# Storing attention rows one round later, interleaving the load halves, and starting the weight loads at round 18

## The chip, the cores and the metric

The kernel runs on one core of one Trainium2 chip. Its five engines work side by side and meet through semaphores: TensorE (PE, matrix products; its weight loads are listed apart as PEld), VectorE (DVE), ScalarE (ACT), GpSimd (POOL) and SyncE (SP), which here only issues DMAs. The metric is the device time of one execution in microseconds (us). The kernel before has a median of 1035.58 us over three runs (1028.32, 1035.58 and 1047.32).

## The reference

The program is a chunked attention followed by two mixture-of-experts layers.

1. Attention: 4 batches, 8 heads, 768 tokens, head size 64, in float32. Each chunk of 32 queries sees 8 memory keys, 16 keys to the left of the chunk, its own 32, and 8 to the right; softmax with scale 1/8; then the weighted sum of the values.
2. The result, as 3072 tokens of 512 numbers, goes through a noisy top-2 router (8 experts, `x @ w1[e]`, relu, `@ w2[e]`, inner size 1024) and the two experts' outputs are added with their weights.
3. That goes through a second layer of 8 experts, with one expert for each token.

## The kernel before, in words

**Tiles and rounds.** The 3072 tokens are cut into 24 tiles of 128. The attention is a software pipeline of 26 rounds, the loop over `t` in `build` (a "round" below is one pass of this loop). Round t does, in this order: `scores(t)` on PE with the maximum and the subtraction on DVE (lines 316 to 325), `flip(t-1)` (PE transposes, copied out by ACT), `exp(t)` on ACT, a piece of `route` (the first router, mostly DVE) in some rounds, `values(t-2)`, `spread(t)` (POOL copies inside the loaded tile), `turn(t-3)` (PE transposes of the finished rows, line 383) and `logits(t-4)`.

**values(t).** PE multiplies the weights with the values (L356). Then SP is given the five loads of tile t+5 (L293), since the tile's buffer is now free: there are five input buffers, `LK = 5`. DVE normalises (L362 to L365) and writes the high half of the row in float16 into a buffer `w`, named x16 (L369, called "the cast" below); POOL writes the low half (L370); SP stores both to `X16` in DRAM (L376, printed as X<-x). There are two x16 buffers, so the cast of tile t writes what tile t-2 used, and it has to wait until the store of tile t-2 has read it.

**Queues.** All these DMAs are issued by SP in program order. An instruction that waits holds back every DMA behind it. The order of the work on every engine is the order in which the Python code emits it. Each SP transfer takes one of eight semaphores in turn (DMAHW0 to DMAHW7 in the order listings) and waits, before it is issued, for the transfer that used that semaphore eight places earlier.

**Weights.** `Weights.fill` loads an expert's weights as eight pieces of 128 x 1024 float32 into four `stage` buffers (L74). From round 24 on, ACT and DVE turn a piece into two float16 halves (L127, L128), which frees its buffer and lets the next load start. The expert products (L543 and L554) follow; their first needs the first pieces of expert 0.

**The first rounds.** Round 2 also makes a table `wide` for the router (DVE), a tile of zeros, and three stores of zeros to `L` and `G` (L1280, L1281).

**The last two tiles** (22 and 23) are not transposed by PE: SP issues a DMA transpose of the row (L373), which needs POOL's half, and then the store.

Of the kernel before, what the change touches and what calls it, by code (L numbers as in the profile page):

```python
# [23 lines left out]
QN, KN, VN = 512, 736, 1040  # L24
QK = QN + KN
VC = VN // 4
XK, XQ, XU, XV = VN, VN + KN, VN + QK, VN + QK + QN
# [227 lines left out]
class Attention:  # L255
# [30 lines left out]
    def load(self, t):  # L286

        x = self.X[t % LK]  # L290
        for i, (p, n, o, e) in enumerate(((0, 32, 0, XU), (32, 32, 3 * VC, XU), (64, 64, XK, XQ),
                                          (64, 32, XU, XV + VN), (96, 32, XU, XV + VC))):
            self.nc.sync.dma_start(x[p:p + n, o:e], self.qkv[i][t])  # L293

    def spread(self, t):
# [48 lines left out]
    def values(self, t):  # L344
        nc, wk, g = self.nc, self.wk, self.g
        x = self.X[t % LK]
        y = self.ET.pop(t)
        o = self.ps.tile([128, 2, 512], F32, name="o")
        for a in range(2):
            for u in range(2):  # L350
                for ch in range(4):
                    i = (D + 1) * (4 * ch + 2 * a + u)
                    v = x[:, i:i + D + 1]
                    v = bass.AP(tensor=v.tensor, offset=v.offset, ap=[v.ap[0], [XV + (3 - 2 * ch) * VC, 2], v.ap[1]])
                    j = 64 * (ch % 2) + 32 * u
                    nc.tensor.matmul(o[32 * ch:32 * ch + 32, a, 130 * u:130 * u + 130],  # L356
                                     y[:, 2 * (ch // 2) + a, j:j + 32], v, start=True, stop=True)
        if t + LK < NT:
            self.load(t + LK)
        o = o[:, :, 0:260].rearrange("p a (h d) -> p a h d", h=4)  # L360
        r = wk.tile([128, 2, 4, 1], F32, name="r")
        nc.vector.tensor_scalar(r, o[:, :, :, D:D + 1], 1e-9, 1.0 / SX, op0=OP.add, op1=OP.mult)  # L362
        nc.vector.reciprocal(r, r)
        x = wk.tile([128, 2, 4, D], F32, name="x", bufs=2)
        nc.vector.tensor_tensor(x, o[:, :, :, 0:D], r.to_broadcast([128, 2, 4, D]), op=OP.mult)  # L365
        xp = x.rearrange("p b a d -> p (b a d)")
        w = g.rr.tile([128, 2, 4, 128], F16, name="x16", bufs=2)
        wf = w.rearrange("p a k q -> p (a k q)")
        nc.vector.tensor_copy(wf[:, :DM], xp)  # L369
        nc.gpsimd.tensor_tensor(wf[:, DM:], xp, wf[:, :DM], op=OP.subtract)  # L370
        y = self.XT[t] = g.rr.tile([128, 2, 4, 128], F16, name="xt", bufs=3)
        if t >= NT - 2:
            nc.sync.dma_start_transpose(out=y.rearrange("p a k q -> p (a k) q"), in_=wf)  # L373
        else:
            self.W[t] = w
        self.stores.append(nc.sync.dma_start(rows(g.X16, t), wf))  # L376

    def turn(self, t):
        nc = self.nc
        w = self.W.pop(t).rearrange("p a k q -> p (a k) q")  # L380
        p = self.ps.tile([128, 512], F32, name="xp").bitcast(F16).rearrange("p (i q) -> p i q", i=8)
        for i in range(8):
            nc.tensor.transpose(p[:, i, :], w[:, i, :], self.g.ident16)
        nc.scalar.activation(self.XT[t].rearrange("p a k q -> p (a k) q"), p, AF.Copy)
# [129 lines left out]
def rows(x, t):  # L514

    return x.rearrange("(u p t) d -> u p t d", u=2, t=M)[t // M, :, t % M]
# [712 lines left out]
def build(tc, xa, xb, xc, xd, xe, noise, wr, wg2, w1, w2, v1, v2, out):  # L1229
    nc = tc.nc  # L1230
    with ExitStack() as top:
        top.enter_context(tc.manual_schedule())
        g = G()
# [16 lines left out]
        def src(e):  # L1250
            v = (w1[e].rearrange("(p k) f -> p (k f)", k=4), w2[e].rearrange("(p k) d -> p (k d)", k=8))
            return lambda i, c: v[i][:, c * 1024:c * 1024 + 1024]

        with ExitStack() as ctx:
            wk = ctx.enter_context(tc.tile_pool(name="wk", bufs=2))
            ld = ctx.enter_context(tc.tile_pool(name="ld", bufs=1))
            at = Attention(tc, g, (xa, xb, xc, xd, xe), ld, wk)
            at.ps = ctx.enter_context(tc.tile_pool(name="psa", bufs=1, space=PSUM))
            at.load(0)
            nc.scalar.preload_act_table_set("natural_log_exp_and_others")  # L1260
            gates = at.gates(noise, wr)
            at.clear(0)
            constants(tc, g, ld)
            for t in range(1, LK):
                at.load(t)
            route = None
            for t in range(NT + 2):
                if t + 1 < LK:
                    at.clear(t + 1)
                if t == 0:  # L1270
                    next(gates)
                if t == 3:
                    at.wrh = next(gates)
                if t == 2:
                    g.wide = g.c.tile([128, 128, M], F16, name="wide")
                    nc.vector.tensor_copy(g.wide, g.iota[:, 0:128, None].to_broadcast([128, 128, M]))
                    z = ld.tile([128, NT * E], F32, name="zero")
                    nc.vector.memset(z, 0.0)
                    for u in range(2):
                        nc.sync.dma_start(g.L.rearrange("(u p t) x -> u p (t x)", u=2, p=128)[u], z)  # L1280
                    nc.sync.dma_start(g.G.rearrange("(p t) x -> p (t x)", p=128), z[:, 0:2 * NT])  # L1281
                if t >= 14:
                    W.depth = min(W.depth + 1, 4)
                    if t == 14:
                        for e in range(E):
                            W.add((1, e), src(e))
                    W.fill()
                if t < NT:
                    at.scores(t)
                if 0 < t <= NT:  # L1290
                    at.flip(t - 1)
                if t < NT:
                    at.exp(t)
                if route and t < 25:
                    for _ in range(2 if t in (17,22) else 1):
                        next(route, None)
                if t >= 2:
                    at.values(t - 2)
                if t < NT:
                    at.spread(t)  # L1300
                if 0 <= t - 3 < NT - 2:
                    at.turn(t - 3)
                if t >= 4:
                    at.logits(t - 4)
                if t >= 4 and (t - 4) % TB == TB - 1:
                    route = at.route((t - 4) // TB)
                    next(route)
                if t == 20:
                    m1 = Moe1(tc, g, dr)
                    m1.gather(0)  # L1310
                if t == 22:
                    for b in range(m1.preps(0)):
                        m1.prep(0, b)
                if t >= 24 and W.may():
                    W.high()
                    W.low(nc.vector)
            m1.gates(0)
# [143 lines left out]
def layouts(inp):  # L1461
# [4 lines left out]
    def split(x, y):  # L1466

        return x.reshape(B, 2, 2, 2, *y)

    def pad(a):  # L1470
        p = np.zeros((B, H, S + 40, D), f)
        p[:, :, 16:16 + S] = a
        return p
    q = split(inp["q"], (TB, 4, 32, D)).transpose(0, 4, 2, 7, 6, 1, 3, 5).reshape(NT, 128, QN)
    p = pad(inp["k"])
    k = np.stack([np.concatenate([x for c in range(4) for x in (p[:, :, 128 * j + 32 * c:128 * j + 32 * c + 32],
                                                                 inp["mem_k"])]
                                 + [p[:, :, 128 * j + 128:128 * j + 152]], axis=2) for j in range(TB)], axis=2)
    k = split(k, (TB, KN // 4, D)).transpose(0, 4, 2, 6, 1, 3, 5).reshape(NT, 128, KN)
    p = pad(inp["v"])  # L1480

    def values(w, c):
# [6 lines left out]
    vb = values(np.concatenate([x for j in range(TB) for x in (p[:, :, 128 * j + 128:128 * j + 152], inp["mem_v"])],  # L1489
                               axis=2), 1)  # L1490
    seq = [b * TB + j for b, j in SEQ]
    k, q, va, vb = k[seq], q[seq], va[seq], vb[seq]
    vu = va[:, 32:].reshape(NT, 32, 4, VC)[:, :, ::-1].reshape(NT, 32, VN)
    qkv = [np.concatenate(x, axis=2) for x in ((va[:, 0:32], k[:, 0:32], q[:, 0:32]),
                                               (vb[:, 0:32], k[:, 32:64], q[:, 32:64]), (k[:, 64:],),
                                               (q[:, 64:96], vu), (q[:, 96:], vb[:, 32:]))]

    def rows(w):

        w = w.reshape(E, 4, 128, 128, 8).transpose(0, 2, 1, 4, 3)  # L1500
        return np.ascontiguousarray(w).reshape(E, DM, F)
# [40 lines left out]
```

## Time and profile before

| | us |
|---|---|
| median of three runs | 1035.58 |
| lowest and highest run | 1028.32, 1047.32 |
| profiled execution, its own time | 1033.13 |
| span of its profile | 1031.4 |
| PE busy in that span | 951.9 |
| DVE, ACT, POOL busy | 504.7, 386.3, 479.4 |

The attention takes the first 147 us or so, the first expert layer ends near 670 us, the second takes the rest. The profile's span is 1.7 us shorter than the time of its own execution. A timeline row gives the start (us from the span's start), the duration, the engine, the line, the operation and its operands; "SPq" rows are the issue of a DMA and not its transfer. A bracket at the end gives how long the engine was idle before, and what ended that idle time.

### The profile page before, as it was taken

Reading aid. Unit: us, or ns where it says so; the run is one execution under the profiler, and the core shown is the slowest. Engines: PE = TensorE matmul, PEld = TensorE weight load, DVE = VectorE, ACT = ScalarE, POOL = GpSimd, SP = SyncE. Lnnn points to the kernel's source line nnn. Section 1 sums busy time; section 2 is a strip of 40 time slices with the busy share of each in tenths; the row PEclk is TensorE's granted clock in tenths of the full one; section 3 lists DMA queues with packets and bytes.
Section 4 is the critical chain, followed back from the end, with each engine's and each line's share of the span. In section 5 each row is a group of like instructions: output and inputs, shape, how many; then the busy total and the mean of one; then the engine's idle time right before and its main releaser. Section 6 shows DMA issues by size and latency. Waiting matters only on the chain.

```text
span 1031.4 us, 18755 instructions
## 1 busy us (share of the span) xinstructions
PE 951.9 (92%) x7259; PEld 566.5 (55%) x7259; DVE 504.7 (49%) x1032; ACT 386.3 (37%) x653; POOL 479.4 (46%) x484
## 2 busy tenths in 40 slices
PE   5897868999989999999999999985889999999998
PEld 4786745656545555455554555542457555555665
DVE  7689885642423443244332443473475436565511
ACT  2453444322323343333433343252423345454421
POOL 6755653334545454645546354335522635443421
PEclk9998969999999999999999999988899999999999
DMA  9999959745746686678766676489535879987720
GB/s 214 253 258 256 237 137 273 178 90 121 189 100 172 164 186 158 154 169 190 170 160 162 152 177 143 131 256 194 96 121 147 219 184 263 287 217 211 148 56 19
DMA packets 189218, 180.75 MB, mean 175 GB/s; under 512 B 152148, under 2 KB 153044, under 8 KB 188352
## 3 DMA queue, kind: packets, MB, share of 16 engines
q1 hardware_dynamic: 166736, 131.24, 54.2%
q0 software_dynamic: 21952, 48.07, 15.8%
q8 instruction: 60, 0.98, 0.4%
q14 instruction: 38, 0.31, 0.1%
q10 hardware_dynamic: 432, 0.15, 0.1%
HBM read 118.27 MB, written 39.53 MB: 153 GB/s over the span
## 4 chain that ended last, share of the span: by engine, by line
PE 41%; issue 16%; POOL 8%; DMA 4%; DVE 2%; ACT 0%; POOLq 0%; DVEq 0%; ACTq 0%
PE ph L543 19%; PE py L554 19%; POOL x L1049 2%; POOL xp L1018 2%; POOL out_dram L1068 2%; POOL gs L1018 2%; DMA stage<-in_v_dram 1%; PE py L736 1%; DMA xp<-Y,ter 1%; DMA xp<-Y,tbr 1%; DMA gs<-Pa,ter 1%; DMA out_dram<-y,teo 0%; DVE hT L546 0%; DMA xt<-x 0%; DVE w L128 0%
## 5 line engine op out<-in xcount | busy, mean ns | idle before, releaser
L543 PE MATMUL ph<-xT,w 128*128 128x384 f16 (+3 forms) x2688 | 426.5, 318 | 19.9 <-DVE hT L546 10.4
L554 PE MATMUL py<-w,hT 128*128 128x512 f16 x1800 | 394.2, 379 | 0.0
L543 PEld LDWEIGHTS <-w 128*128 128x128 f16 x2688 | 262.5, 99 | 166.8 <-issue 24.5
L554 PEld LDWEIGHTS <-hT 128*128 128x128 f16 x1800 | 175.7, 98 | 207.0
L546 DVE SCALAR_TENSOR_TENSOR hT<-ph,hT 128x384 f16<-128x384 f32 (+3 forms) x224 | 115.9, 521 | 218.0 <-ACT hT L545 216.9
L128 DVE SCALAR_TENSOR_TENSOR w<-stage,w 128x1024 f16<-128x1024 f32 x128 | 167.2, 1309 | 66.5 <-ACT w L127 66.3
L545 ACT ACTIVATE hT<-ph 128x384 f16<-128x384 f32 (+3 forms) x224 | 103.3, 463 | 212.6 <-PE ph L543 209.0
L127 ACT ACTIVATE w<-stage 128x1024 f16<-128x1024 f32 x128 | 133.6, 1049 | 19.1 <-DMA stage<-in_v_dram 14.3
L654 ACT ACTIVATE y<-py,gs 128x512 f32<-128x512 f32 x48 | 32.9, 686 | 176.4 <-PE py L554 170.3
L657 POOL DMA_INDIRECT L<-l,t3y x43 | 44.5, 1035 | 109.6 <-DVE l L686 106.2
L675 DVE SCALAR_TENSOR_TENSOR x<-y,x 128x512 f16<-128x512 f32 x50 | 34.4, 688 | 123.0 <-ACT x L671 122.9
L657 POOL DMA_INDIRECT Y<-y,t3y x43 | 44.8, 1041 | 91.5 <-ACT y L654 85.7
L1068 POOL DMA_INDIRECT out_dram<-y,tbo x20 | 20.8, 1039 | 110.8 <-ACT y L1067 89.0
L316 PE MATMUL s<-x 128*64 128x64 f32 x768 | 49.6, 287 | 16.3 <-DMA x<-in_xe_dram 11.6
L611 POOL DMA_INDIRECT Y<-ol,late x48 | 56.4, 1175 | 16.4 <-issue 16.4
L316 PEld LDWEIGHTS s<-x 128*64 128x64 f32 x768 | 46.3, 209 | 17.8 <-POOL x L303 8.3
L1067 ACT ACTIVATE y<-py,gs 128x512 f32<-128x512 f32 x27 | 18.6, 687 | 94.8 <-PE py L554 64.1
L370 POOL TENSOR_TENSOR x<-x,x 128x512 f16<-128x512 f32 x24 | 29.4, 1226 | 45.8 <-DVE x L369 25.1
L585 POOL DMA_INDIRECT xg<-X,t3x x43 | 42.0, 976 | 15.1 <-issue 14.6
L585 POOL DMA_INDIRECT gs<-G,t3g x41 | 38.7, 944 | 12.5 <-issue 12.5
L303 POOL COPY x<-x 24x780 f32<-24x780 f32 x48 | 41.0, 855 | 5.2 <-issue 2.5
L1049 POOL TENSOR_TENSOR x<-xp 128x512 f32<-128x512 f32 x27 | 35.9, 1355 | 15.1 <-DVE xg L1052 11.7
(276 smaller groups left out, 708.1 us busy)
## 6 DMA issues: line engine op xcount, KB each, us to landing
stage<-in_w_dram SPq DMA_DIRECT2D x64, 512.0 KB, 4.1
stage<-in_v_dram SPq DMA_DIRECT2D x64, 512.0 KB, 5.1
x<-in_xa_dram SPq DMA_DIRECT2D x24, 286.0 KB, 5.5
X<-x SPq DMA_DIRECT2D x24, 256.0 KB, 4.4
x<-in_xd_dram SPq DMA_DIRECT2D x24, 194.0 KB, 6.7
x<-in_xb_dram SPq DMA_DIRECT2D x24, 188.5 KB, 6.6
x<-in_xc_dram SPq DMA_DIRECT2D x24, 184.0 KB, 6.0
x<-in_xe_dram SPq DMA_DIRECT2D x24, 96.5 KB, 5.6
```

What stands on the lines that cost most here:

```text
L127: nc.scalar.activation(hi, src, AF.Copy, scale=SW)
L128: return lambda v=nc.vector: v.scalar_tensor_tensor(lo, src, SW, hi, op0=OP.mult, op1=OP.subtract)
L316: nc.tensor.matmul(s[o:o + 64, ch // 2, b], q[:, b, ch], k[:, b, 40 * ch:40 * ch + 64], start=True, stop=True)
L543: nc.tensor.matmul(p[:, :n], w1[:, a, k, f, :], xT[:, b, k, :n], start=(i == 0), stop=(i == 11))
L545: nc.scalar.activation(hT[:, 0, f, :n], p[:, :n], AF.Relu)
L546: nc.vector.scalar_tensor_tensor(hT[:, 1, f, :n], p[:, :n], 0.0, hT[:, 0, f, :n], op0=OP.max, op1=OP.subtract)
L554: nc.tensor.matmul(p[:m], hT[:, a, f, o:o + m], w2[:, c, f, :], start=(i == 0), stop=(i == 23))
L585: self.nc.gpsimd.indirect_dma_start(out=out, out_offset=None, in_=src, in_offset=IO(ap=idx, axis=0))
L611: st = nc.gpsimd.indirect_dma_start(out=self.Y, out_offset=IO(ap=idx[:, i:i + 1], axis=0), in_=z, in_offset=None, bounds_check=2 * N - 1, ...
L657: st = nc.gpsimd.indirect_dma_start(out=dst, out_offset=IO(ap=idx, axis=0), in_=src, in_offset=None, bounds_check=2 * N - 1, oob_is_err=False)
L1049: nc.gpsimd.tensor_tensor(s, x[:, :DM], x[:, DM:], op=OP.add)
L1068: st = nc.gpsimd.indirect_dma_start(out=self.out, out_offset=IO(ap=idx, axis=0), in_=y, in_offset=None, bounds_check=N - 1, oob_is_err=False)
```

## The change

1. The store of a tile's rows moves out of `values(t)` into a new method `keep`, which `turn(t)` calls in the next round. For tiles 22 and 23, which have no `turn`, it stays in `values`, behind the DMA transpose.
2. The five loads of a tile are issued in another order, so that they alternate between partitions 0 to 63 and 64 to 127. Their sizes are as before.
3. The table `wide` and the zero stores move from round 2 to round 6.
4. The first weight loads move from round 14 to round 18: one in each of rounds 18 to 21, where it was 14 to 17.

```diff
-        for i, (p, n, o, e) in enumerate(((0, 32, 0, XU), (32, 32, 3 * VC, XU), (64, 64, XK, XQ),
-                                          (64, 32, XU, XV + VN), (96, 32, XU, XV + VC))):
+        for i, (p, n, o, e) in enumerate(((0, 32, 0, XU), (64, 32, XU, XV + VN), (32, 32, 3 * VC, XU),
+                                          (64, 64, XK, XQ), (96, 32, XU, XV + VC))):
             self.nc.sync.dma_start(x[p:p + n, o:e], self.qkv[i][t])
...
         if t >= NT - 2:
             nc.sync.dma_start_transpose(out=y.rearrange("p a k q -> p (a k) q"), in_=wf)
+            self.keep(t, wf)
         else:
             self.W[t] = w
-        self.stores.append(nc.sync.dma_start(rows(g.X16, t), wf))
+
+    def keep(self, t, wf):
+        self.stores.append(self.nc.sync.dma_start(rows(self.g.X16, t), wf))
 
     def turn(self, t):
         nc = self.nc
         w = self.W.pop(t).rearrange("p a k q -> p (a k) q")
+        self.keep(t, w.rearrange("p i q -> p (i q)"))
...
-                if t == 2:
+                if t == 6:
                     g.wide = g.c.tile([128, 128, M], F16, name="wide")
...
-                if t >= 14:
+                if t >= 18:
                     W.depth = min(W.depth + 1, 4)
-                    if t == 14:
+                    if t == 18:
                         for e in range(E):
                             W.add((1, e), src(e))
```

On SP, in the first rounds: the loads of tile 7 (buffer x_90) and the store behind them. In `X_62<-x_501` the first name is the array X16 and the second the row buffer's tile; x_501 is tile 2, x_414 is tile 1.

```order
 L293 DMA x_90<-in_xa_dram 32x2288
-L293 DMA x_90<-in_xb_dram 32x1508
-L293 DMA x_90<-in_xc_dram 64x736
-L293 DMA x_90<-in_xd_dram 32x1552
+L293 DMA x_90<-in_xb_dram 32x1552
+L293 DMA x_90<-in_xc_dram 32x1508
+L293 DMA x_90<-in_xd_dram 64x736
 L293 DMA x_90<-in_xe_dram 32x772
-L376 DMA X_62<-x_501 128x1024
+L379 DMA X_62<-x_414 128x1024
```

The inputs' names are dealt out anew with the order: what was in_xd is in_xb now. The place behind the five loads of tile 7 belonged to the store of tile 2 and now belongs to that of tile 1.

On SP, at the end of the attention: rounds 22 to 24, after the last loads. The old numbers x_2146, x_2263, x_2364 and x_2429 are tiles 19, 20, 21 and 22; the new x_2145, x_2262, x_2363 and x_2428 are the same tiles. `xT<-xg` are the transposes for the first expert group, `xt<-x_2429` is the transpose of tile 22.

```order
-L376 DMA X_62<-x_2146 128x1024
-L376 DMA X_62<-x_2263 128x1024
-L642 DMA_TRANSPOSE xT<-xg 128x8x128 x2
-L376 DMA X_62<-x_2364 128x1024
-L373 DMA_TRANSPOSE xt<-x_2429 128x8x128
-L376 DMA X_62<-x_2429 128x1024
...
+L379 DMA X_62<-x_2145 128x1024
+L646 DMA_TRANSPOSE xT<-xg 128x8x128 x2
+L379 DMA X_62<-x_2262 128x1024
+L373 DMA_TRANSPOSE xt<-x_2428 128x8x128
+L379 DMA X_62<-x_2428 128x1024
+L379 DMA X_62<-x_2363 128x1024
```

The store of tile 21 stood ahead of the transpose and the store of tile 22; now it stands behind both. The group's two transposes stand one store earlier.

On DVE, what stands around the cast of tile 23, x_2479, in the changed kernel (tile 23 writes the x16 buffer of tile 21); `w_71<-stage` are conversions of expert 0's first weights.

```order
L363 RECIPROCAL r<-r 128x8 [waits DVE_49]
L365 TENSOR_TENSOR x<-o,r 128x512 [waits DVE_49,Pool_49]
L369 CAST x_2479<-x 128x512 [waits DMAHW2_49,DMAHW3_49,DVE_49,Pool_49]
L128 SCALAR_TENSOR_TENSOR w_71<-stage,w_71 128x1024 [waits Activation_49]
L251 SCALAR_TENSOR_TENSOR wg_2518<-wg2f,wg_2518 128x32 [waits DMAHW5_49,Activation_49]
```

The order of these instructions is as before; the cast waited for one transfer (DMAHW2) and now waits for two (DMAHW2 and DMAHW3).

## Rows read from the trace of the kernel before

**Rows 1.** Windows by stage: length, busy us and (xinstructions) of each engine, PEclk, DMA share, GB/s.

```profile
0.00:30.00 30.00, 14.04 (x228) 12.34 (x230) 23.14 (x48) 7.39 (x18) 20.72 (x54) 0.99 0.97 217
30.00:58.00 28.00, 28.00 (x526) 24.87 (x522) 17.83 (x40) 14.30 (x32) 20.34 (x23) 0.95 1.02 256
58.00:118.00 60.00, 51.70 (x923) 44.92 (x920) 53.72 (x170) 24.88 (x56) 32.01 (x35) 0.94 0.97 256
146.00:220.00 74.00, 63.79 (x438) 41.32 (x439) 47.52 (x141) 25.79 (x44) 29.56 (x26) 0.91 0.79 210
220.00:660.00 440.00, 437.31 (x2717) 230.96 (x2715) 153.11 (x252) 156.06 (x248) 215.88 (x208) 1.00 0.65 153
```

**Rows 2.** Waits of PE, 0 to 30 us: total, times, longest.

```profile
PE s L316 <- DMA x<-in_xe_dram: 11.2, 3, 8.3
```

**Rows 3.** Waits of PE, 30 to 118 us.

```profile
PE misc L227 <- DVE two L428: 3.9, 1, 3.9
PE s L316 <- DMA x<-in_xe_dram: 0.4, 1, 0.4
```

**Rows 4.** Waits of the SP queue, 30 to 118 us.

```profile
SPq L376 <- POOL x L370: 10.3, 10, 3.5
SPq L293 <- DMA stage<-in_w_dram: 4.0, 3, 1.7
```

**Rows 5.** Timeline, 50 to 57 us.

```profile
50.85 0.34 SPq L376 DMA_DIRECT2D X<-x  x1
...
51.66 2.08 PE L316 MATMUL s<-x 128*64 128x64 f32 x32
...
54.51 0.31 SPq L293 DMA_DIRECT2D x<-in_xe_dram  x1
...
55.86 0.34 SPq L376 DMA_DIRECT2D X<-x  x1
...
56.08 2.07 PE L316 MATMUL s<-x 128*64 128x64 f32 x32
...
56.80 0.43 DVE L369 CAST x<-x 128x512 f16<-128x512 f32 x1 [0.18 <-DMA X<-x]
```

**Rows 6.** The tile X (the array X16): its stores' landing.

```profile
DMA to landing us min/median/max: 2.1/4.4/6.9
```

**Rows 7.** Timeline, 86 to 125 us: SP issues and casts.

```profile
87.80 0.34 SPq L376 DMA_DIRECT2D X<-x  x1
...
88.92 0.92 DVE L369 CAST x<-x 128x512 f16<-128x512 f32 x1
...
120.73 0.42 SPq L293 DMA_DIRECT2D x<-in_xe_dram  x1
...
124.40 0.84 DVE L369 CAST x<-x 128x512 f16<-128x512 f32 x1
```

**Rows 8.** Timeline, 139 to 149 us: the end of the attention.

```profile
139.17 0.34 SPq L376 DMA_DIRECT2D X<-x  x1
...
143.97 1.91 POOL L370 TENSOR_TENSOR x<-x,x 128x512 f16<-128x512 f32 x1 [2.21 <-DVE x L369]
...
145.91 1.25 SPq L373 DMA_TRANSPOSE xt<-x  x1
...
146.67 0.43 DVE L369 CAST x<-x 128x512 f16<-128x512 f32 x1
...
147.01 1.22 DVE L128 SCALAR_TENSOR_TENSOR w<-stage,w 128x1024 f16<-128x1024 f32 x1
147.20 0.58 SPq L376 DMA_DIRECT2D X<-x  x1
...
148.29 0.82 PE L543 MATMUL ph<-xT,w 128*128 128x256 f16 x3 [0.33 <-DVE w L128]
```

**Rows 9.** DMA summary, 0 to 30 us.

```profile
DMA packets 2472, 6.52 MB, mean 217 GB/s; under 512 B 822, under 2 KB 1206, under 8 KB 2267
```

**Rows 10.** DMA summary, 30 to 80 us.

```profile
DMA packets 4292, 12.94 MB, mean 259 GB/s; under 512 B 993, under 2 KB 993, under 8 KB 3940
```

**Rows 11.** Timeline, 18 to 22 us: the table and the zeros of round 2.

```profile
18.40 0.96 DVE L1276 COPY wide<-iota 128x1536 f16<-128x1536 f16 x1
19.35 0.22 DVE L1278 MEMSET zero<- 128x192 f32 x1
...
20.04 1.27 SPq L1280 DMA_DIRECT2D L<-zero  x2
```

More of the change, by code (lines that the diff above doesn't have):

```diff
@@ L1494, in layouts @@
     qkv = [np.concatenate(x, axis=2) for x in ((va[:, 0:32], k[:, 0:32], q[:, 0:32]),
-                                               (vb[:, 0:32], k[:, 32:64], q[:, 32:64]), (k[:, 64:],),
-                                               (q[:, 64:96], vu), (q[:, 96:], vb[:, 32:]))]
+                                               (q[:, 64:96], vu),
+                                               (vb[:, 0:32], k[:, 32:64], q[:, 32:64]),
+                                               (k[:, 64:],), (q[:, 96:], vb[:, 32:]))]
     def rows(w):
```

## The prediction, as it was made before the result

> **What bounds the kernel now.** I read the windows by stage first, because an average over the span hides that the change touches only the first 147 us. In [rows 1] the stretch from 220 to 660 us has PE busy for 437.31 of 440.00 us, so a microsecond lost or won before 220 us is not made good later: it arrives at the end nearly whole. From 30 to 58 us PE is busy for all of 28.00 us while the DMA share is 1.02: two resources are full, and PE is the one that sets the pace. From 58 to 118 us DVE takes over, with 53.72 of 60.00 us (the router's pieces lie there), and the DMA share is still 0.97. So the DMA rings are full for 118 us, which invites the reading that the loads are the bound.
>
> The waits say otherwise. Up to 30 us PE waits 11.2 us for the last of a tile's loads, 8.3 of it the very first tile [rows 2]. From 30 to 118 us it waits for a load only 0.4 us, and its longest wait, 3.9 us, is for a router step on DVE [rows 3]. Five input buffers hide the full rings. What is visible on SP is another matter: there stores wait 10.3 us for POOL, ten times, and hold the loads behind them [rows 4]; but a load that is late and still in time costs PE nothing.
>
> **The change part by part.**
>
> *The store one round later, as SP sees it.* It removes the 10.3 us of waits for POOL [rows 4]: a round later POOL's half is long there. The following loads move up by about 1 us each. Worth at the end: at least nothing, at most the 0.4 us that PE waits for loads there [rows 3]. I take 0.4 us won.
>
> *The store one round later, as DVE sees it.* There are two row buffers, so the cast of tile n waits for the store of tile n-2. Before, that store was issued two rounds ahead, and one cast shows how tight this was: the store issued at 50.85 us was just being waited for at 56.80 us, with 0.18 us of idle time [rows 5]. Now the store stands where the next tile's stood. In this round that is 55.86 us, or 54.51 + 0.31 = 54.82 us if it need not wait for POOL. With the median landing of 4.4 us [rows 6] it lands at 59.2 to 60.3 us, so this cast comes 2.4 to 3.5 us late. Queued behind the cast on DVE are the maximum and the subtraction of the next tile; ACT waits for those, and PE for ACT's exponentials, but only in the next round but one. A round lasts 56.08 - 51.66 = 4.4 us [rows 5], so PE can run on while DVE falls behind by up to about one round, and the stretch from 30 to 58 us has 28.00 - 17.83 = 10.2 us of DVE idle time to take part of it [rows 1]. The lateness doesn't add up round by round there. But DVE becomes the bound at 58 us, and what it brings along of lateness is then paid. Bounds: 0 (all hidden) and 3.5 us. I take 1.5 us, nearer to the lower half because the rings hold one store less by then.
>
> Two later places have the same pattern. The cast at 88.92 us: the store that it will wait for gets the place of the one at 87.80 us [rows 7], lands 4.4 us later at 92.2, so 3.3 us late; but the weight piece of that round is gone, and DVE has been working without a break, which gives the store time. The cast at 124.40 us: its store follows the load issued at 120.73 + 0.42 = 121.15, lands at 125.6, 1.2 us late. Bounds for the two together 0 and 4.5 us; I take 1 us.
>
> *The end of the attention.* This is the place I am surest of. The cast of tile 23, at 146.67 us, writes the buffer of tile 21. Before, the store of tile 21 went out at 139.17 us. Now it stands on SP behind the DMA transpose of tile 22, which cannot go before POOL has finished that tile's half at 143.97 + 1.91 = 145.88 us, and behind that tile's store at 147.20 us, whose issue takes 0.58 us [rows 8]. So the store of tile 21 goes out at 147.8 us and lands 2.1 to 4.4 us later [rows 6], at 149.9 to 152.2 us. The cast is late by 3.2 to 5.5 us, and behind it on DVE stands the conversion of the first weights (147.01 us), for which PE waits at 148.29 us [rows 8]. SP is held as well: the transpose of tile 23 needs POOL after that cast, and the next weight loads stand behind it. Nothing that I see covers this, since 146 to 220 us has PE idle for 74.00 - 63.79 = 10.2 us [rows 1] for want of converted weights. Bounds: 0, if the weights' landing and not their conversion sets the pace there, and 5.5 us. I take 3.5 us lost, nearest to the rows of a lightly loaded queue.
>
> *The alternating loads.* The first 30 us, nearly all loads, moved 217 GB/s [rows 9]; from 30 to 80 us, with the 128-partition stores among them, it was 259 GB/s at the same full share [rows 10]. So loads into half the partitions run slower than the rings could. If alternation brought the first 30 us to 259 GB/s, their 6.52 MB would take 25.2 us instead of 30: up to 4.8 us won, and not less than 0. Only waits in the start count (11.2 us, [rows 2]), the first of which, 8.3 us, needs all five loads of one tile anyway. I take 1 us won.
>
> [...]
>
> *The table and the zeros.* 0.96 + 0.22 us on DVE leave round 2, and 1.27 us of issue leave SP [rows 11]. In round 6 DVE has the idle time named above, so they cost nothing there; without that cover they would cost the 1.2 us again. Won: 0.2 us, bounds 0 and 1.2, since scores of that round ended only shortly before.
>
> *The weights.* Four pieces leave rounds 14 to 17, where the loads waited 4.0 us for them on SP [rows 4], and join the last loads in rounds 18 to 21. They are needed only in round 24. PE waited for no load in either place; won at most the 0.4 us already counted, lost at most as much as SP waited, 4.0 us, if the last tiles' loads come late. I take 0.
>
> **Sum.** -0.4 + 1.5 + 1.0 + 3.5 - 1.0 - 0.2 = +4.4 us on the profiled execution's own 1033.1 us (span 1031.4): 1037.5 us, say **1037 us**. That execution lies 2.5 us under the median of the three runs, well inside their spread of 1028.3 to 1047.3. Before and after differ by less than that spread: 2%, or 20.7 us, is what a measurement of this kernel can tell from no change.
>
> **The rivals.**
>
> *The rings were the bound after all (faster).* For it: the DMA share of 1.02 and 0.97 [rows 1] and the two rates [rows 9, 10]. If freed queues and alternating halves shorten the landing, the casts don't wait (0 instead of 2.5), the start gives 4.8 and the table 1.2, with 0.4 for the loads; against that the tail stays. 3.5 - 4.8 - 1.2 - 0.4 = -2.9 us, and with the tail hidden too -6.4: 1027 to 1030 us. Against it: the 0.4 us of [rows 3]. A gain over 2% would need 20.7 us, which no wait for DMAs in [rows 2 to 4] holds.
>
> *The cast becomes the loop (slower).* One mechanism: in every round the cast waits for a store that was issued only after the loads of the round before, and the store goes out only after PE's values, which hang two rounds later on that cast. Its place is the stretch from 30 to 58 us, 28.00 / 4.4 = 6 rounds. It decides when the landing takes so long that DVE is more than one round (4.4 us) late: at the largest landing seen, 6.9 us [rows 6], the cast of [rows 5] comes at 54.82 + 6.9 = 61.7, 4.9 us late, just past that point. If the 3.5 us were then paid in all 6 rounds, that is 21 us, and with the tail 24: 1058 us. Half absorbed, 10 to 12 us: about 1047 us.
>
> *Nothing moves.* PE and DVE hide the DMA edits, and the weights' landing hides the tail: 1033 us. The order of issue shows that the edits do reach the queues, so only the covers could do this.
>
> **How the numbers follow.** Chances: the forecast (1 to 8 us lost) 0.50, the faster rival 0.27, no move 0.10, the slower rival 0.13, of which about half is over 2%. The runs' own spread, 7.3 us down and 11.7 up from the median, comes on top of each. The low end is the lowest run before less the faster rival's 5 us or so, 1023; the high end is between the highest run, 1047.3, and that run with the forecast's 4.4 us, 1050. Most of the slower rival's tail is left out. Faster by over 2%: 0.03, which only scatter could bring; slower by over 2%: 0.07; the same: 0.90.
>
> **What would show it.** Right: casts after an idle time ended by a store (X<-x) in many rounds up to 58 us and at tile 23, where the first conversion of weights then starts 3 us or more after the cast's old place; SP's waits of stores for POOL nearly gone; PE's first expert product later against the last scores than before. Wrong: if casts wait for nothing, the DVE terms fall; if the first 30 us move clearly more than 217 GB/s and the tile spacing there shrinks, the loads were worth more; if PE waits for loads in rounds 21 to 23, the weights came at the wrong time.

## The result, and the profile after

The changed kernel has a median of 1053.72 us over 20 runs (1043.89 to 1062.33). The kernel before, run 20 times beside it on the same chip, has 1042.76 us (1028.32 to 1047.32). Both hold some slower executions at the upper end; without them the ratio of after to before is 1.0148, with a 95% interval of 1.0124 to 1.0172. That is 13 to 18 us of 1040: slower, by less than 2%. Forecast were 1037 us and a range from 1023 to 1050 us, so the time lies outside the range, on the side that the forecast named.

| | before | after |
|---|---|---|
| span of the profile, us | 1031.4 | 1057.6 |
| PE busy, us | 951.9 | 962.5 |
| DVE, ACT, POOL busy, us | 504.7, 386.3, 479.4 | 501.4, 383.5, 478.4 |
| start of the last tile's cast, us | 146.67 | 160.65 |
| first products of the fifth expert group, us | 262.2 | 276.0 |

The busy times of DVE, ACT and POOL did not grow. PE's did, by 10.6 us for the same 7259 products; its clock is taken up in the last section. The last two rows tell where the time is: the attention ends 14.0 us later, and the fifth group of expert products (the fifth set of tokens that goes through an expert) still starts 13.8 us later, close to the measured ratio. What the two spans differ by beyond that comes later in single executions, and these scatter: the lowest and the highest run before lie 19 us apart. The rest of this text therefore compares the starts of casts and groups.

The windows of after, as [rows 1] has them of before:

```profile
0.00:30.00 30.00, 14.90 (x234) 13.03 (x235) 21.48 (x46) 7.40 (x18) 20.98 (x54) 1.00 0.97 223
30.00:58.00 28.00, 25.79 (x474) 22.28 (x471) 15.51 (x35) 12.33 (x26) 17.35 (x20) 0.94 0.89 233
58.00:118.00 60.00, 49.31 (x846) 42.92 (x844) 49.55 (x159) 24.29 (x56) 32.38 (x35) 0.91 0.82 213
146.00:220.00 74.00, 56.81 (x445) 37.85 (x446) 48.31 (x136) 28.44 (x46) 27.26 (x23) 0.86 0.73 192
220.00:660.00 440.00, 427.73 (x2616) 224.47 (x2616) 148.75 (x257) 147.34 (x238) 211.73 (x206) 0.99 0.64 152
```

From 30 to 118 us every column fell but one (POOL in the third stretch): PE is no longer busy throughout the second stretch (25.79 of 28.00), DVE lost 4 us in the third, and the DMA share fell to 0.82. No resource is full any more; something makes them wait. The first stretch moved a little more, 223 GB/s for the 217 of [rows 9].

What it is, the view of the cast's line (DVE, L369) says: the idle time of DVE just before it, in us and number of times, and what ended it.

```profile
  DMA X<-x: 17.5, 8
  issue: 3.6, 1
```

Before, this was 0.2 us, once [rows 5]. Now nine casts wait 21.1 us in all; eight of the waits the profile puts down to a store of rows. For the ninth it names no releaser, but in the trace this cast (tile 19) waits for the same semaphore that the store of tile 17 carries, so it is a store's too. The timeline shows three places. First the round of tile 5, two tiles ahead of the one in [rows 5]:

```profile
48.19 0.35 SPq L379 DMA_DIRECT2D X<-x  x1
...
50.90 0.58 SPq L293 DMA_DIRECT2D x<-in_xe_dram  x1
...
51.58 0.37 SPq L379 DMA_DIRECT2D X<-x  x1
51.88 0.43 DVE L369 CAST x<-x 128x512 f16<-128x512 f32 x1 [2.62 <-DMA X<-x]
52.23 0.69 DVE L323 TENSOR_REDUCE m<-s 128x8 f32<-128x512 f32 x1
...
53.02 0.69 DVE L325 TENSOR_TENSOR d<-s,m 128x512 f32<-128x512 f32 x1
...
53.74 0.82 ACT L333 ACTIVATE e<-d 128x256 f32<-128x256 f32 x3 [1.72 <-DVE d L325]
```

The store of 48.19 us has landed at about 51.85; until then the cast stands, and behind it in DVE's order stand the maximum (L323) and the subtraction (L325) of another tile, for which ACT then waits 1.72 us. So the wait passes from the row buffer to DVE, to ACT, and on to PE. Tiles 3, 5, 6 and 7 wait 1.1 to 2.6 us each, 8.0 us in all; tile 7, the one of [rows 5], waits 1.12 us. Not all of that is lost. DVE's longest waits for the scores of PE in the stretch of tiles 2 to 7, before (30 to 58 us) and after (30 to 62 us):

```profile
DVE m L323 <- PE s L316: 4.1, 4, 1.1
DVE s L321 <- PE s L316: 3.0, 2, 1.9
...
DVE s L321 <- PE s L316: 2.0, 1, 2.0
DVE m L323 <- PE s L316: 1.6, 2, 1.0
```

These waits shrank from 7.1 to 3.6 us, so idle time that was there before took up part of the new one, and the tiles behind run 3.9 us late against before.

The second place answers to the first rows of [rows 7], tile 13:

```profile
88.30 0.34 SPq L483 DMA_DIRECT2D G<-gt  x1
...
90.62 0.58 SPq L293 DMA_DIRECT2D x<-in_xe_dram  x1
91.30 0.37 SPq L379 DMA_DIRECT2D X<-x  x1
...
92.14 0.69 DVE L365 TENSOR_TENSOR x<-o,r 128x512 f32<-128x512 f32 x1
...
96.47 0.43 DVE L369 CAST x<-x 128x512 f16<-128x512 f32 x1 [3.64 <-DMA X<-x]
```

The router's store to G waits on SP until DVE has made its numbers (6.3 us, in SP's waits below), and the five loads and the store of tile 11 stand behind it. Before, the store of tile 11 went out ahead of the one to G:

```profile
82.58 0.34 SPq L376 DMA_DIRECT2D X<-x  x1
...
84.36 0.33 SPq L479 DMA_DIRECT2D G<-gt  x1
```

Now it goes out at 91.30 us, behind it, and lands 5.1 us later.

The third place is one that the prediction saw only in part, tiles 17 to 19, where the weights now begin:

```profile
123.68 0.43 DVE L369 CAST x<-x 128x512 f16<-128x512 f32 x1 [0.81 <-DMA X<-x]
...
124.49 0.37 SPq L379 DMA_DIRECT2D X<-x  x1
126.26 0.35 SPq L74 DMA_DIRECT2D stage<-in_w_dram  x1
...
129.98 0.35 SPq L379 DMA_DIRECT2D X<-x  x1
130.07 0.43 DVE L369 CAST x<-x 128x512 f16<-128x512 f32 x1 [2.02 <-DMA X<-x]
...
136.65 0.43 DVE L369 CAST x<-x 128x512 f16<-128x512 f32 x1 [3.65 <-issue]
```

The cast of tile 18 (130.07) comes 5.6 us behind the issue of the store that it needs (124.49), that of tile 19 (136.65) 6.7 us behind its own (129.98). Three casts in a row wait 6.5 us together. The end, against [rows 8]:

```profile
156.82 1.24 SPq L373 DMA_TRANSPOSE xt<-x  x1
158.12 1.04 SPq L379 DMA_DIRECT2D X<-x  x2
159.26 0.40 SPq L74 DMA_DIRECT2D stage<-in_w_dram  x1
160.65 0.43 DVE L369 CAST x<-x 128x512 f16<-128x512 f32 x1 [3.10 <-DMA X<-x]
160.99 1.22 DVE L128 SCALAR_TENSOR_TENSOR w<-stage,w 128x1024 f16<-128x1024 f32 x1
...
162.27 0.82 PE L547 MATMUL ph<-xT,w 128*128 128x256 f16 x3 [3.39 <-DVE w L128]
```

This is as forecast: the stores of tiles 22 and 21 stand together behind the transpose, the cast waits 3.10 us, the first conversion behind it is late, and PE waits 3.39 us for it, where it waited 0.33.

How the lateness grows can be read from the casts of tiles 8, 12 and 22, behind the first place, ahead of the second, and behind the third. Before, then after:

```profile
63.93 0.43 DVE L369 CAST x<-x 128x512 f16<-128x512 f32 x1
85.96 0.43 DVE L369 CAST x<-x 128x512 f16<-128x512 f32 x1
143.31 0.43 DVE L369 CAST x<-x 128x512 f16<-128x512 f32 x1
...
67.86 0.43 DVE L369 CAST x<-x 128x512 f16<-128x512 f32 x1
89.90 0.43 DVE L369 CAST x<-x 128x512 f16<-128x512 f32 x1
154.22 0.43 DVE L369 CAST x<-x 128x512 f16<-128x512 f32 x1
```

Tiles 8 and 12 are 3.9 us late, tile 22 10.9 and tile 23 14.0. So the first place costs 3.9 us for 8.0 us of idle time at the casts, the second and third together 7.0 for 10.1, and the end 3.1 for 3.1.

On SP the waits of [rows 4] have gone and others stand in their place (30 to 118 us, the two longest):

```profile
SPq L293 <- PE o L356: 26.8, 11, 8.6
SPq L483 <- DVE cm L487: 6.3, 1, 6.3
```

No store waits for POOL's half of the row any more (10.3 us before), and the loads wait mostly for PE to free a buffer (26.8 us; 5.8 before): the loads are ahead of the work and are not what is missing. PE waits for no load at all from 30 to 130 us.

### The profile page after: what moved, and what is told of

Read it like the earlier page. It is cut to its first block, busy times and chain, and to the rows that moved or that the text cites. A ratio compares the mean times of both kernels' runs of the same rounds, so it can differ in the third digit from the quotient of the medians.

```text
span 1057.6 us, 18771 instructions
## 1 busy us (share of the span) xinstructions
PE 962.5 (91%) x7259; PEld 570.2 (54%) x7259; DVE 501.4 (47%) x1032; ACT 383.5 (36%) x653; POOL 478.4 (45%) x484
## 4 chain that ended last, share of the span: by engine, by line
PE 38%; issue 17%; POOL 8%; DMA 4%; DVE 2%; ACT 1%; POOLq 0%; SPq 0%; DVEq 0%; ACTq 0%
PE py L558 19%; PE ph L547 17%; POOL x L1053 2%; POOL xp L1022 2%; POOL gs L1022 2%; POOL out_dram L1072 2%; DMA xt<-x 2%; DMA stage<-in_v_dram 1%; PE py L740 1%; DMA xp<-Y,tbr 1%; ACT w L127 1%; DMA gs<-Pa,ter 1%; DVE w L128 0%; DVE hT L550 0%; PE lg L240 0%
## 5 line engine op out<-in xcount | busy, mean ns | idle before, releaser
L547 PE MATMUL ph<-xT,w 128*128 128x384 f16 (+3 forms) x2688 | 430.9, 320 | 21.6 <-DVE hT L550 9.1
L1072 POOL DMA_INDIRECT out_dram<-y,tbo x20 | 20.8, 1040 | 113.9 <-ACT y L1071 95.8
L589 POOL DMA_INDIRECT xg<-X,t3x x43 | 42.0, 976 | 15.1 <-issue 14.6
```

What stands on the lines that cost most here:

```text
L547: nc.tensor.matmul(p[:, :n], w1[:, a, k, f, :], xT[:, b, k, :n], start=(i == 0), stop=(i == 11))
L589: self.nc.gpsimd.indirect_dma_start(out=out, out_offset=None, in_=src, in_offset=IO(ap=idx, axis=0))
```

## The experiments

Ratios are to the kernel before, measured beside each on the same chip, with 95% intervals; not all experiments ran on the same chip. Four theories were named in the expectations: **W**, the casts wait for the stores that come a round later, and DVE pays; **D**, the order of the loads, or the weights, makes the landing longer; **L**, the landing of the weights sets the pace at the end; **C**, one lag made in the first rounds is carried on, and the later waits follow from it.

**The store alone.** Before, with `keep` and its calls from the change (part 1 of the diff), and nothing else.

> Only the store moves to the next round; loads, table and weights as before. Theory W (the cast of tile n waits for the store of tile n-2, and DVE pays): casts sit idle before a landing store 12 to 25 us in total, the last cast starts at 156 to 162 us (146.7 before, 160.7 in the change), ratio to before 1.009 to 1.016. Rival D (the new load order and the later weights lengthen the landings, the store is innocent): idle time before casts under 4 us, last cast before 152 us, ratio at most 1.005.

Ratio 1.0149 (1.0087 to 1.021). The cast's line, idle time ended by a store:

```profile
  DMA X<-x: 23.7, 11
```

The last cast starts at 163.4 us, 16.7 later than before and a little beyond the 156 to 162 us that W gave. This one move makes the whole loss.

**Everything but the store.** After, with the store back in `values`:

```diff
-            self.keep(t, wf)
...
-    def keep(self, t, wf):
-        self.stores.append(self.nc.sync.dma_start(rows(self.g.X16, t), wf))
+        self.stores.append(nc.sync.dma_start(rows(g.X16, t), wf))
...
-        self.keep(t, w.rearrange("p i q -> p (i q)"))
```

> The change without its store part: alternating loads, table in round 6, weights from round 18, store as before. Theory W: no idle time before casts beyond 2 us, last cast 143 to 149 us, ratio to before 0.995 to 1.003. Rival D: last cast at 152 us or later and ratio 1.005 or more.

Ratio 0.9974 (0.9939 to 1.0009). The cast's line:

```profile
  DMA X<-x: 0.9, 1
```

The last cast starts at 147.1 us and the fifth group at 261.5 (before 146.7 and 262.2). Loads, table and weights together cost nothing.

**A third row buffer.** After, with the store late as in the change, but the cast of tile n waits for the store of tile n-3.

```diff
...
-        w = g.rr.tile([128, 2, 4, 128], F16, name="x16", bufs=2)
+        w = (self.ld.tile([128, 2, 4, 128], F16, name="x16c") if t % 3 == 2 else
+             g.rr.tile([128, 2, 4, 128], F16, name="x16", bufs=2))
```

> The whole change, but with a third row buffer in the attention, so the cast of tile n waits for the store of tile n-3. (To make room one start-up integer table shares its space with another.) Theory W: idle time before casts under 3 us, last cast 143 to 149 us, ratio to before 0.994 to 1.003. Rival D: the third buffer changes little, last cast after 154 us, ratio over 1.008.

(All three kernels with a third buffer also share the start-up table that the expectation names, and what that does by itself was not measured.)

No cast waits (idle 0), the last starts at 148.0 us, and the fifth group at 261.9. The ratio, 1.004 (1.0003 to 1.0077), is a little above what was expected. The late stores stand where they did; only the reuse of their buffers has been put off, and the lateness in the attention and at the fifth group is gone. So the buffer is what made them costly up to there. For the whole time this is less clear. Against the kernel above (0.9974) 0.7% may be left for the late store as such; their intervals just touch. Against the kernel with three buffers and the store back in `values` (0.9955, below, on another chip) it is 0.8%, and the intervals don't overlap. At the fifth group the three lie within 1.2 us, so what is left would come behind it; no run here shows where.

**The weights back at round 14.**

```diff
-                if t >= 18:
+                if t >= 14:
...
-                    if t == 18:
+                    if t == 14:
```

> The change with the weight loads back in rounds 14 to 17. Theory W with the weight pieces as a second cause: the idle time before the casts of tiles 17 to 19 (0.8, 2.0 and 3.7 us in the change) falls to under 4 us in sum, that at tiles 13 to 16 grows; last cast 156 to 160 us; ratio to before 1.009 to 1.015. Rival D (the weights' new place is the cause): last cast before 152 us, ratio at most 1.005.

Ratio 1.0135 (1.0078 to 1.0193). The waits of DVE from 113 to 150 us, where after has 2.8 + 3.6 us at the casts:

```profile
DVE x L369 <- DMA X<-x: 3.8, 2, 2.5
```

The last cast starts at 158.8 us instead of 160.7. So the weight pieces among the stores of rounds 18 to 21 cost about 2 us of the loss in these two executions (2.6 us of waits, 1.9 at the last cast); the ratios' intervals overlap and don't tell the two kernels apart.

**Three parts of the late store, one at a time.** After, with `late(t)` true for a group of tiles only; the others are stored in `values`. Effective are tiles 0 to 7, tiles 8 to 20, and tile 21.

```diff
-            self.keep(t, wf)
...
+        if not late(t):
+            self.keep(t, wf)
...
-        self.keep(t, w.rearrange("p i q -> p (i q)"))
+        if late(t) and late(t + 1):
+            self.keep(t, w.rearrange("p i q -> p (i q)"))
```

(For the first two groups `late` holds for one tile more, and that tile is stored ahead of the next `values`, so that no store is left behind. For tile 21 the condition is `late(t)` alone.)

> The change, with the late store for tiles 0 to 7 alone; from tile 8 on the store stands where it stood before. Theory W (every late store is paid at its own place): casts idle 6 to 10 us in total, all up to tile 9; the cast of tile 10 at 77.5 to 79 us as in the change (74.55 without the store part); last cast 150 to 152 us; ratio to before 1.000 to 1.005. Rival C (one lag is made in the first rounds and carried on, the later waits follow from it): last cast at 157 us or later, ratio over 1.009.

> The change, with the late store for tiles 8 to 20 alone. Theory W: idle time before the casts near tile 13 (3 to 4 us) and tiles 17 to 19 (5 to 7 us in sum), last cast 153 to 158 us, ratio to before 1.004 to 1.010. Rival C: last cast before 150 us, ratio under 1.003.

> The change, with the late store for tile 21 alone: its store stands behind the transpose and the store of tile 22. Theory W: one idle time, 3 to 4 us, before the last cast, which starts at 150 to 151 us; no other cast waits over 1 us; ratio to before 0.999 to 1.004 (3 us are 0.3%). Rival L (the landing of the weights sets the pace of the first expert group, the cast's lateness is hidden): the second expert group starts no later than without the store part (179.5 us), ratio 0.994 to 0.999.

| late tiles | ratio, interval | idle at casts, us | last cast, us | fifth group, us |
|---|---|---|---|---|
| none (the kernel above) | 0.9974, 0.9939 to 1.0009 | 0.9 | 147.1 | 261.5 |
| 0 to 7 | 0.9992, 0.9949 to 1.0034 | 7.4 | 150.2 | 267.2 |
| 8 to 20 | 1.0057, 1.0013 to 1.01 | 11.3 (1.0 of it at tiles 6 and 7) | 155.9 | 268.9 |
| 21 | 0.9996, 0.9954 to 1.0038 | 3.8 (0.7 of it at tile 6) | 149.7 | 262.9 |
| all (after) | 1.0148, 1.0124 to 1.0172 | 21.1 | 160.7 | 276.0 |

At the last cast the three groups bring 3.1, 8.8 and 2.6 us over the kernel without late stores. Part of that is there before any store can matter: the first casts of the first two executions come 0.7 and 1.5 us later than that kernel's, and the first cast of after 0.5. Less these starts the three bring 2.4, 7.3 and 2.6 us, together 12.3, where after has 13.1. At the fifth group they bring 5.7, 7.5 and 1.4 us, together 14.6, where after has 14.5; that these fit so closely is luck, since the distance from the last cast to the fifth group lies anywhere between 111 and 117 us in the executions profiled here. Within that the places add up, and the lateness of one is not swallowed by the next: W holds. C doesn't: it had the last cast at 157 us or later for tiles 0 to 7 and before 150 for tiles 8 to 20, and they came at 150.2 and 155.9.

With tile 21 alone late, L had the second expert group no later than the 179.5 us of the kernel without late stores. It starts at 180.4, so L doesn't hold either, but 0.9 us of the cast's 2.6 is little: PE's next waits, for DVE and for the second group's rows, were 1.3 and 0.8 us shorter in this execution.

The ratios alone (0.2%, 0.8% and 0.2% over the first row) sum to 1.2%, where after lies 1.7% over it. Their intervals are as wide as that difference, and the first row was measured on another chip than the three groups.

**No late store, and three buffers.** After with both edits.

> The change without its store part and with a third row buffer in the attention. Theory W: the one wait that was left without the store part (0.9 us at the cast of tile 7) goes, last cast 145.5 to 147 us, ratio to before 0.993 to 1.000. Rival (a third buffer is worth as much as the loads' new order and more, since PE is free to run ahead): last cast before 144 us, ratio under 0.993.

Ratio 0.9955 (0.9918 to 0.9992), no idle time at the casts, as expected. The last cast starts at 148.0 us, later than expected, in an execution whose first cast came at 23.2 us instead of 21.5. A third buffer adds nothing that can be measured where the stores go out early.

**The late stores on ACT's queue.** After, and the kernel with three buffers, with

```diff
-        self.stores.append(self.nc.sync.dma_start(rows(self.g.X16, t), wf))
+        q = self.nc.scalar if t < NT - 2 else self.nc.sync
+        self.stores.append(q.dma_start(rows(self.g.X16, t), wf))
```

The question was whether the place behind the loads on the one queue makes the stores late (W1) or the round's delay alone (W2).

> The change, but the late stores (tiles 0 to 21) are issued by ACT in the same later round, so they don't stand behind that round's five loads on SP. Theory W1 (what makes the store late for the cast is its place behind the loads of its round on the one queue): idle time before casts falls from 21 us to under 8 us, the last cast starts at 147 to 153 us (160.7 in the change), none of the 3 us at tile 23 is left, ratio to before 0.998 to 1.006. Rival W2 (the round's delay alone does it, on any queue, since the rings are full): idle time over 14 us, last cast after 156 us, ratio 1.008 or more. Side effect to look for: ACT itself may wait for a semaphore that a load still holds, and hold its copies.

> As the run before, with a third row buffer too. Both theories: no cast waits; last cast 145 to 149 us; ratio to before 0.993 to 1.002. Over 1.004 would show that the issue on ACT costs by itself.

No cast waits for a store in either, as W1 said. But neither theory had the time: 1.0177 (1.0119 to 1.0235) and 1.0187 (1.0121 to 1.0252), last casts at 167.1 and 169.0 us. The waits of SP in act_late, 30 to 118 us:

```profile
SPq L293 <- DMA X<-x: 38.8, 12, 5.9
```

and of PE in the same stretch:

```profile
PE s L316 <- DMA x<-in_xe_dram: 8.2, 6, 2.5
PE s L316 <- issue: 5.1, 1, 5.1
```

Now loads wait for stores, though a load shares no buffer with a store of rows. What they share is the eight semaphores that this program deals out to these transfers in turn: ACT issues its store only after its own earlier work (that of 71.00 us behind a copy at 68.68 us, for which ACT had waited 6.22 us for PE), and the load that comes eight places later can't be issued before that store has landed. In the trace the store that ACT issues at 71.00 us and the load that waits for it until 73.20 us carry the same semaphore. So the two queues are tied together, and the wait has moved from DVE to PE. Since the casts came late for another reason here, W1 against W2 isn't settled by these two runs.

**The alternating loads alone.** Before, with the new order of the five loads and of their inputs.

```diff
-        for i, (p, n, o, e) in enumerate(((0, 32, 0, XU), (32, 32, 3 * VC, XU), (64, 64, XK, XQ),
-                                          (64, 32, XU, XV + VN), (96, 32, XU, XV + VC))):
+        for i, (p, n, o, e) in enumerate(((0, 32, 0, XU), (64, 32, XU, XV + VN), (32, 32, 3 * VC, XU),
+                                          (64, 64, XK, XQ), (96, 32, XU, XV + VC))):
...
```

> The kernel before with the loads' new order alone. If the order shortens the start: the first 30 us move over 225 GB/s (217 before), the cast of tile 0 starts 0.3 to 1 us earlier; last cast 145.5 to 147.5 us, ratio to before 0.996 to 1.001, since a POOL step holds PE in the fourth round anyway. If the loads were the bound: last cast before 144 us, ratio under 0.995.

Ratio 0.9946 (0.9903 to 0.9988), the lowest of the eleven, and faster than both kernels. The expectation was missed: it had 0.996 to 1.001 and an earlier first cast, which starts at 22.4 us (22.3 before). A ratio under 0.995 it gave to loads that are the bound, but with a last cast before 144 us, and that comes at 146.4. The DMA summary of its first 30 us:

```profile
DMA packets 2544, 6.81 MB, mean 227 GB/s; under 512 B 839, under 2 KB 1223, under 8 KB 2322
```

227 GB/s for 217 [rows 9], 5% more. Yet the last cast starts only 0.3 us earlier than before; the larger difference comes behind it, 3.3 us at the second group of expert products and 4.5 at the fifth. Why the first expert layer runs shorter isn't shown by any run here. Its interval and that of the kernel without late stores and with three buffers overlap; which of the two is better stays open.

## Why the prediction was wrong, step by step

**Right: the mechanism, its places and its sign.** The cast waits for a store issued a round later, DVE holds what is queued behind it, and at the end PE waits for the conversion. The rows of the cast and of the tail in after show it, the kernel with three buffers shows that the lateness up to the fifth group comes by the buffer, and the kernel with the store alone that this part of the change makes the whole loss.

**The step that failed** is the size of the cast waits before the end: "The lateness doesn't add up round by round there", with 1.5 us for 30 to 58 us and 1 us for the two later places. Measured are 3.9 us for the first (tiles 8 to 12 of after against before; 2.4 with tiles 0 to 7 alone late) and 7.0 us for the second (tile 12 to tile 22; 7.3 with tiles 8 to 20 alone late). Together that is 10.9 us for 2.5. It failed at three points.

- *One cast was looked at where several wait.* From 30 to 58 us the text costed the cast of tile 7 alone, at 3.5 us at most. Tiles 3, 5, 6 and 7 waited, 8.0 us in all. For the cast at 124.40 us it had 1.2 us, with the median landing of 4.4 us [rows 6]. There were three, tiles 17, 18 and 19, with 6.5 us, and two of them waited for stores that took 5.6 and 6.7 us to release them. The moved weight pieces, taken at 0, are part of it: about 2 us.
- *The cover was counted at more than it was worth.* The 10.2 us of idle DVE time in [rows 1] are there, and DVE's waits for PE did shrink by 3.5 us; that left 3.9 of 8.0 us to be paid, where the text had 1.5 of 3.5. Behind that, where DVE was busy for 53.72 of 60.00 us up to 118 us [rows 1], 7.0 of 10.1 us were paid.
- *The price was right and was then marked down.* For the cast of tile 13 the text had 3.3 us from the place of the store; measured are 3.6 us of idle time and 2.6 us more lateness. Then 1 us was taken for this place and the next together, on account of the weight piece that has gone and of DVE's other work. Neither kept the cast from waiting: five loads and the G store, which itself waits for DVE, stood ahead of the store.

**The end of the attention**, 3.5 us: 3.1 of idle time, 2.6 at the last cast with this store alone late. Right in size up to that cast; but at the fifth group only 1.4 us of it are left in that execution. The reason given, that PE's 10.2 us of idle time from 146 to 220 us are for want of converted weights, was misread. Before, PE's waits for the conversion there are

```profile
PE ph L543 <- DVE w L128: 2.0, 3, 1.4
```

and the rest is for other things, some of which did cover a part.

**The alternating loads**, 1.0 us won: the rate of the first 30 us is up from 217 to 223, 225 and 227 GB/s in the whole change, the change without the late store, and the loads alone, 3 to 5%; up to the last cast, 0.3 us with the loads alone. The bound of 4.8 us, which took the 259 GB/s of [rows 10] for the start, falls. Alone this part won 0.5% (0.1 to 1.0%), more than the 1.0 us, but where the forecast did not look for it, behind the attention.

**SP's waits for POOL**, 0.4 us won: they went, as forecast, and brought nothing that shows, since the loads were in time anyway (from 30 to 118 us PE waited for them 0.4 us before and not at all after). **Table and zeros**, 0.2 us won: not told apart from the other edits; with all of them the fifth group starts 0.7 us earlier than before. **Weights** against PE: it waited for no load in rounds 21 to 23, as forecast; their cost came by the stores instead.

**The rivals.** The rings were not the bound: with the casts free and the loads, the table and the weights as in the change, the ratio is 0.9974, at most 0.6% of a gain (0.9939). The slower rival, in which the cast becomes the loop, named the right resource; its lesser case, 10 to 12 us from half-absorbed waits and then the tail, 1047 us on a base of 1033, is near what happened. That is partly luck, since the casts wait in nine rounds and not in every one, and mostly after 58 us and not before.

**The base.** The profiled execution of before, 1033.1 us, turned out low: only one of the 20 runs before was shorter. The sum was made on it, so the time missed by two things: the kernel before takes longer than that execution, and the change costs 13 to 18 us where the sum had 4.4.

## What to carry to other kernels

Before a store is moved later, look up which instruction next writes its buffer, where the store will then stand on its queue and what waits ahead of it there, and add the landing of that stretch, not the median of all. If that instruction stands on the engine that sets the pace, price every such instruction and not one of a kind, and add the places up. Idle time that the engine had before covered only part of it here: half of the waits were paid where DVE had idle time, 7 of 10 us where it was nearly full, and all of it at the last cast. One more buffer took the wait away here with the store still late: no cast waited, and the last started at 148.0 us instead of 160.7.

## What the runs showed that I had not expected

- Issuing the stores from ACT tied SP's loads to ACT's progress here: 38.8 us of SP waits in 88 us, up to 5.9 us each, through semaphores that are dealt out in turn and not through any data.
- The landing of the same kind of store differs from place to place: 3.7 us at 48 us, 5.1 at 91, and up to the cast 5.6 and 6.7 at 124 and 130, where a weight piece is issued behind the store (126.26 and 130.38 us). With the pieces back at round 14 the casts from 113 to 150 us wait 3.8 us instead of 6.4.
- PE's mean granted clock over the whole attention was 0.92 of full speed in after (0 to 160 us), for 0.94 before (0 to 146); in the last 14 us of each it was 0.74 and 0.75. PE was busy 117.19 us over the whole attention, for 112.90 before, with nearly the same count of products (2035 and 2030). What this adds to the loss isn't separated by any run here. The 0.86 of the window from 146 to 220 us above is no sign of a slower expert layer: in after that window holds the end of the attention, and from 160 to 234 us the clock is 0.91, as before.
- What comes behind the fifth group scatters from one execution to the next. On one and the same chip, the kernel with the late store alone had a profile span of 1030.1 us, and the kernel without late stores, whose attention ends 16.3 us earlier, one of 1030.7. Two single spans can't tell two such kernels apart.
